# Four scalars in one tile, a filler at the top of memory, weight loads two steps later and more generator steps in the first chunk

## The chip, the cores and the metric

One Trainium2 chip, one of its cores. The metric is the device time of one execution of the whole program in microseconds; three runs were timed, and one more execution was profiled. "TensorE" multiplies matrices, "VectorE", "ScalarE" and "GpSimd" work on elements, and "SyncE" issues most of the DMA transfers from its queue, called SP below.

## The reference

Three layers in a row, on float32 data; batch 4, sequence 576, model width 512 (8 heads of 64).

```python
# attention, per head; only scores within tau of the row's maximum stay
scores = scale * q @ k.T
scores = where(scores >= max(scores) - tau, scores, -1e9)
attn = softmax(scores);  x = attn @ v
# mixing over the sequence (rank 32), then a two-matrix block of width 2048
u = x + ((x.T @ U) @ V).T
x = u + relu(u @ w_ch1) @ w_ch2
# gate: causal convolution of 5 taps, sigmoid
out = (sigmoid(conv(x, conv_w)) * (x @ w_val)) @ w_out
```

U, V and the weight matrices arrive as 64-bit floats and are converted on the chip.

## The kernel before

**Stages.** Attention runs first, in 144 slots `s` of 128 query rows (`9 * NP`), with TensorE taking turns at scores, transposes and attention times values. Then comes the dense part: the hidden width of 2048 is worked off in four chunks c = 0..3 of 512 columns. Chunk 0 is plain: `h1` (L902) and `ch` (L960), each by five blocks of up to 512 of the 2304 rows, with matmuls of 512 columns. Chunks 1 to 3 run over three groups j of 768 rows: `first_layer` (L1122) has seven items of 12 matmuls of 384 columns (a product scheme that gets by with seven block products instead of eight), `second_layer` (L1165) has eight groups of 12. Every float32 product is made of three matmuls (high by high, high by low, low by high). The output stage is `val` (L1039) and `proj` (L1068).

**Operands.** The seven operands of a group j are spilled to DRAM during chunk 0 (`spill`, and `combos`, whose lines are L868 to L877) and fetched again by `fetch` (L1097, DMA at L1101) into four places in turn. A fetch is given out when an item has been used, four items ahead.

**Weights.** A row of weights is loaded into one of two buffers `raw` (L159 for `weight_rows`, L182 for `stage_rows`), converted from 64-bit floats in seven operations (`from_f64`: ScalarE at L102, VectorE at L104, L107, L111, L115, L125, GpSimd at L130), and split into a high part (L171, ScalarE) and a low part (L173, GpSimd). For the first matrix of chunks 1 to 3, `combine` (L189 to L209) forms seven sums of blocks instead. L125 is the last reader of `raw`; the next load into that buffer waits for it in the SP queue, and everything behind it on that queue waits too.

**Order.** All of this is written by hand as Python generators: `work.tick()` (L219) takes each of at most four live generators one step further, which means one operation or a pause, and then starts the next in line. So the number of ticks between two matmul groups sets where each operation stands in its engine's queue. Before a load, `wstage` (L137) waits until the buffer before last has been converted. In chunk 0, `tick` (L1008) is called after each group of 12 matmuls: 24 calls while `lot` is set, which is taken away at L1219, and 8 after it, 32 in all. A first-layer item gives one tick (L1161), a group of the second layer two (L1181). `need` (L808) and L1131 give ticks until the rows are there.

**Memory.** Tiles take whole multiples of 32 bytes per partition, from byte 16,512 upwards in the order of the code: idn 512, then four scalars of 32 each (4 bytes used), cw 96 (80 used), u, ring, w1_0, w2_0 and everything after them, so u begins at 17,248, 96 past a multiple of 256. Pools with `side="right"` are laid out downwards from byte 229,344, which is 224 past a multiple of 256. The sizes of the large tiles are multiples of 256. So before, everything large on the left side begins at 96 past a multiple of 256 (u, w1_0, w2_0, raw, wt, wf, the combined weights w1_s, h2), and on the right side at 224 (the region with its operands, us, w2_1, the tiles of q and k). The identity idn begins at 16,512, 128 past one.

Of the kernel before, what the change touches and what calls it, by code (L numbers as in the profile page):

```python
# [21 lines left out]
F32 = mybir.dt.float32  # L22
# [14 lines left out]
def attention_moe_kernel(  # L37
# [24 lines left out]
    NP = B * H // 2  # L62
# [14 lines left out]
    def f(ap):  # L77
        return ap.bitcast(F32)

    const = ctx.enter_context(tc.tile_pool(name="const", bufs=1))  # L80
    idn = const.tile([128, 128], F32, name="idn")
    tau_sb = const.tile([128, 1], F32, name="tau_sb")
    ntau = const.tile([128, 1], F32, name="ntau")
    tau_eff = const.tile([128, 1], F32, name="tau_eff")
    qscale = const.tile([128, 1], F32, name="qscale")
    cw = const.tile([128, KC, KD], F32, name="cw")
    u = const.tile([128, KD, T], F32, name="u")
    ring = const.tile([128, 1280], F32, name="ring")

    w1_0 = const.tile([128, 2, KD, FC], F32R, name="w1_0")  # L90
    w2_0 = const.tile([128, 2, KD, FC], F32R, name="w2_0")
    wst_p = ctx.enter_context(tc.tile_pool(name="wst", bufs=2))
# [42 lines left out]
    slot = [0]  # L135

    def wstage(n):  # L137
        k = len(started)
        started.append(k)
        while k - len(loaded) >= 2:  # L140
            yield
        raw = wst_p.tile([128, FC, 2], I32, tag="raw", name="raw")
        return raw[:, 0:n, :]
# [104 lines left out]
    work = Staged(4)  # L248
# [13 lines left out]
    def attention(dense_front, dense_mid, dense_back):  # L262
# [388 lines left out]

        nu = 5 * R
        raw_uv = [next_of(wstage(n)) for n in (FC, nu + S - FC)]
        nc.gpsimd.memset(raw_uv[0][:, 0:nu], 0)
        rv = [a.rearrange("p a b -> p (a b)") for a in raw_uv]
# [132 lines left out]
    p1 = {}  # L788
# [54 lines left out]
    def spill(n, t):  # L843
        for j in range(NG):
            for half in range(2):
                a = 2 * G * j + G * half
                lo, hi = max(a, n * NB), min(a + G, n * NB + size[n])
                if lo < hi:
                    for o, k in (((B11, 0), (B21, 2)) if not half else ((B22, 2),)):
                        for p in range(2):  # L850
                            nc.sync.dma_start(
                                out=spilled[j, o][:, p, :, lo - a:hi - a],
                                in_=f(t[:, p, k:k + 2, lo - n * NB:hi - n * NB]))
# [31 lines left out]
    def split_block(src, pool=None):  # L885
        for t in split_steps(src, pool):
            pass
        return t

    def u_src(n):  # L890
        return [(0, size[n], u[:, :, n * NB:n * NB + size[n]])]
# [10 lines left out]
    def h1(c, us, n, apart=False):  # L902
        m = size[n]
        t = p1["h2"] if n == 2 else block_tile(1 + (n + (n > 2)) % 2)
        for e in range(KD):
            ps = p1["a"].tile([128, 512], F32, tag="a", name="a")
            passes(ps, w1[c % 2][0], us, e, m)
            if apart:
                yield t
            nc.scalar.activation(out=t[:, 0, e, 0:m], in_=ps[:, 0:m], func=ACTF.Relu)  # L910
            nc.vector.scalar_tensor_tensor(
                out=t[:, 1, e, 0:m], in0=ps[:, 0:m], scalar=0.0, in1=f(t[:, 0, e, 0:m]), op0=ALU.max, op1=ALU.subtract
            )
            if not apart:
                yield t
# [41 lines left out]
    def dense():  # L957
# [27 lines left out]
        def gate_step():  # L985
            if len(ended) < len(tapped) and tapped[len(ended)] not in gates:
                b, e = tapped[len(ended)]
                g = gate(b, e)
                nc.scalar.activation(out=g, in_=g, func=ACTF.Sigmoid)
                ended.append((b, e))  # L990
            if not gates or gates[0][0] > 1 and "g" not in p1:
                return
            if gates[0] not in tapped:
                return tap(*gates[0])
            b, e = gates[0]
            k = tap_no[0]
            g = gate(b, e, k, S - k)
            nc.vector.scalar_tensor_tensor(
                out=g, in0=u[:, e, b * S:(b + 1) * S - k], scalar=cw[:, KC - 1 - k, e:e + 1], in1=g,
                op0=ALU.mult, op1=ALU.add  # L1000
            )
            if k == 2 and len(gates) > 1 and not (gates[1][0] > 1 and "g" not in p1):
                tap(*gates[1])
            tap_no[0] = k % (KC - 1) + 1
            if k == KC - 1:
                gates.pop(0)

        def tick(n=1):  # L1008
            work.tick()
            turn["w"] ^= 1  # L1010
            if turn["w"] and "lot" not in p1:
                work.tick()
            for _ in range(n):
                gate_step()
            if p1.get("lots"):
                p1["lot"](p1["lots"].pop(0))
# [15 lines left out]
        turn = {"o": 0, "w": 0}  # L1032
# [62 lines left out]
        fetched, used = [], [0]  # L1095

        def fetch(n):  # L1097
            while len(fetched) < min(n, len(stream)):
                _, j, o = stream[len(fetched)]
                t = operands[len(fetched) % 4]  # L1100
                nc.sync.dma_start(out=f(t), in_=spilled[j, o])  # L1101
                fetched.append(t)
# [3 lines left out]
        def low_parts(left=0):  # L1106
            while len(lows) > left:
                src, hi, lo = lows.pop(0)
                nc.vector.scalar_tensor_tensor(  # L1109
                    out=lo, in0=src, scalar=0.0, in1=f(hi), op0=ALU.max, op1=ALU.subtract)  # L1110

        def relu_sum(ps, x, o, k, half):
            hi, lo = (hs[:, a, k, half * G:(half + 1) * G] for a in range(2))
            nc.vector.tensor_tensor(out=o, in0=ps, in1=x, op=ALU.add)  # L1114
            nc.scalar.activation(out=hi, in_=o, func=ACTF.Relu)  # L1115
            lows.append((o, hi, lo))

        def bank(n):
            pool, tag = (c_ps, "c") if n % 2 else (p1["a"], "a")
            return pool.tile([128, 512], F32, tag=tag, name=tag)[:, 0:G]  # L1120

        def first_layer(c, j):  # L1122
            sb = [p1["c"][:, n * G:(n + 1) * G] for n in range(8)]

            def add(ps, x, o):
                nc.vector.tensor_tensor(out=sb[o], in0=ps, in1=sb[x], op=ALU.add)

            for i in range(7):
                t = fetched[used[0]]
                while (c, i) not in summed:  # L1130
                    work.tick()  # L1131
                for m in range(2):
                    ps = bank(m)
                    k = 0
                    for kk in range(2):
                        wh, wl = (parts[i][:, a, kk, m * 128:(m + 1) * 128] for a in range(2))
                        for lhs, rhs in ((wh, t[:, 0, kk]), (wh, t[:, 1, kk]), (wl, t[:, 0, kk])):
                            nc.tensor.matmul(ps, lhs, rhs, start=k == 0, stop=k == 5)  # L1138
                            k += 1
                    if i == 0:  # L1140
                        nc.scalar.activation(out=sb[m], in_=ps, func=ACTF.Copy)  # L1141
                    elif i == 1:
                        add(ps, m, 2 + m)
                    elif i == 2:
                        add(ps, 2 + m, 4 + m)
                    elif i == 3:
                        relu_sum(ps, sb[4 + m], sb[6 + m], 2 + m, 1)
                        add(ps, 2 + m, 2 + m)
                    elif i == 4:
                        relu_sum(ps, sb[2 + m], sb[2 + m], m, 1)  # L1150
                    elif i == 5:
                        relu_sum(ps, sb[m], sb[m], m, 0)
                    else:
                        relu_sum(ps, sb[4 + m], sb[4 + m], 2 + m, 0)
                    low_parts(1)
                used[0] += 1
                if j == NG - 1:
                    freed[0] += 1
                fetch(used[0] + 4)
                for _ in range(1):  # L1160
                    work.tick()  # L1161
                if c == NCH - 1:
                    gate_step()
# [38 lines left out]

        p1["lot"] = lot
        p1["lots"] = [3, 3, 2, 2, 1, 1, 1, 2, 1, 1, 1, 2, 1, 1, 1, 1, 1, 1, 1, 1, 1, 1]
        for n in range(2, NN):
            for t in h1(0, us, n):
                tick()
            held.append((n, t))
            if n + 1 < NN:
                us = split_block(u_src(n + 1))  # L1210
                spill(n + 1, us)
            else:
                fetch(2)
            ch(0, *held.pop(0))
# [75 lines left out]
```

## Time and profile before

| | us |
|---|---|
| median of 3 runs | 837.14 (836.63 to 837.53) |
| the profiled execution | 836.76 |
| its span, first to last instruction | 835.0 |
| TensorE busy | 809.7 (97%) |
| VectorE busy | 682.3 (82%) |
| ScalarE busy | 441.1 (53%) |
| GpSimd busy | 270.2 (32%) |
| mean granted clock of TensorE | 0.993 |

The page gives each engine's busy time as a share of the span, the span in 40 slices, the DMA queues, the chain of work that ended last, and the costliest groups of instructions. Engines are written PE (matmuls), PEld (weight loads into TensorE, beside the matmuls), DVE, ACT, POOL and SP, in the order TensorE, VectorE, ScalarE, GpSimd, SyncE. Matmul records overlap, because the next one starts before the last one's end: the rate is read from one start to the next. A line such as L1176 is a line of the kernel before.

### The profile page before, as it was taken

To read this page: it belongs to the slowest core of one execution; us is meant where nothing else is said; L and a number is where in the kernel's file an instruction comes from. 1 tells how busy PE (TensorE), PEld (TensorE's weight loads), DVE (VectorE), ACT (ScalarE), POOL (GpSimd) and SP (SyncE) were. 2 spreads that over 40 slices of the span, in tenths; PEclk is the share of its full clock that TensorE was granted. 3 is DMA by queue.
4 is the path that set the end of the run, shared out by engine and by line. 5 is a ranking of instruction groups with operands and counts; after the bars stand their busy time and mean duration, and the time that the engine had idled before them with its cause. 6 is when DMAs were issued, how large, how long until landed. Compare 5 with 4: busy or idle time off the path is not lost. (4 is left out here: it accounts for less than half of the span.)

```text
span 835.0 us, 15123 instructions
## 1 busy us (share of the span) xinstructions
PE 809.7 (97%) x5264; PEld 726.3 (87%) x5264; DVE 682.3 (82%) x1414; ACT 441.1 (53%) x929; POOL 270.2 (32%) x362
## 2 busy tenths in 40 slices
PE   8999999999999999999998999999899999999998
PEld 8788888888888887888888998999899999978886
DVE  7999999999999984479977799588896897977740
ACT  6788888888888884344232224213342252344531
POOL 6724523622432420242762167015561310000000
PEclk9999999999999999999999999999989999999999
DMA  7766776685676524476675755559365473001112
GB/s 147 183 145 150 176 166 145 147 185 130 154 169 142 122 50 165 141 266 230 221 271 197 245 191 220 202 179 333 116 266 205 161 265 114 1 1 50 52 51 75
DMA packets 87397, 134.19 MB, mean 161 GB/s; under 512 B 45669, under 2 KB 62837, under 8 KB 87322
## 3 DMA queue, kind: packets, MB, share of 16 engines
q1 hardware_dynamic: 85130, 130.92, 53.1%
q0 software_dynamic: 848, 1.92, 0.9%
q8 instruction: 42, 0.69, 0.3%
q10 hardware_dynamic: 1344, 0.39, 0.2%
q14 instruction: 33, 0.27, 0.1%
HBM read 85.43 MB, written 21.23 MB: 128 GB/s over the span
## 5 line engine op out<-in xcount | busy, mean ns | idle before, releaser
L494 POOL TENSOR_TENSOR th<-nm,tau_eff 128x1 f32<-128x1 f32 x144 | 69.9, 485 | 177.2 <-DVE ns L479 170.2
L504 DVE SCALAR_TENSOR_TENSOR e<-ns,th,e 128x576 f32<-128x576 f32 x144 | 124.3, 863 | 1.4 <-POOL th L494 0.4
L493 ACT ACTIVATE e<-ns,nm 128x576 f32<-128x576 f32 x144 | 112.0, 778 | 20.4 <-DVE ns L479 20.2
L479 DVE TENSOR_SCALAR_CACHE_REDUCE ns<-s 128x576 f32<-128x576 f32 x144 | 107.6, 748 | 9.1 <-PE s L465 8.3
L130 POOL TENSOR_TENSOR wf<-wf,wt 128x512 f32<-128x512 f32 (+2 forms) x43 | 60.7, 1411 | 142.4 <-DVE wt L125 141.7
L465 PE MATMUL s<-st 128*128 128x288 f32 x480 | 93.9, 317 | 0.1
L520 PE MATMUL xm<-idn,e 128*128 128x128 f32 x576 | 86.5, 273 | 2.5 <-DVE e L504 2.4
L1176 PE MATMUL a<-region,w 128*128 128x384 f32 x432 | 84.2, 340 | 4.8 <-ACT w L171 2.1
L1138 PE MATMUL a<-region,w_s 128*128 128x384 f32 x378 | 78.9, 344 | 8.8 <-DMA region<-sp 6.9
L529 ACT ACTIVATE pt<-xm 128x512 f32<-128x512 f32 x144 | 85.7, 595 | 1.6
L1176 PEld LDWEIGHTS a<-region,w 128*128 128x128 f32 x432 | 76.4, 190 | 7.1 <-DVE region L1109 3.2
L1176 PE MATMUL c<-region,w 128*128 128x384 f32 x432 | 81.6, 337 | 0.0
L465 PEld LDWEIGHTS s<-st 128*128 128x128 f32 x480 | 67.9, 189 | 11.9 <-issue 4.2
L1138 PE MATMUL c<-region,w_s 128*128 128x384 f32 x378 | 77.6, 341 | 0.0
L1138 PEld LDWEIGHTS a<-region,w_s 128*128 128x128 f32 x378 | 68.0, 192 | 10.9 <-issue 5.1
L1115 ACT ACTIVATE region<-c_sb 128x384 fp32r<-128x384 f32 x72 | 37.6, 524 | 75.0 <-DVE c_sb L1114 75.0
L1176 PEld LDWEIGHTS c<-region,w 128*128 128x128 f32 x432 | 76.4, 189 | 0.0
L520 PEld LDWEIGHTS xm<-idn,e 128*128 128x128 f32 x576 | 69.3, 140 | 4.4 <-PE s L465 2.3
L574 PE MATMUL o<-pt,vt 128*64 128x256 f32 (+1 forms) x768 | 69.8, 331 | 0.0
L1138 PEld LDWEIGHTS c<-region,w_s 128*128 128x128 f32 x378 | 68.1, 190 | 0.0
L574 PEld LDWEIGHTS o<-pt,vt 128*64 128x64 f32 x768 | 41.4, 137 | 24.5 <-issue 10.3
L102 ACT ACTIVATE wt<-raw 128x512 f32<-128x512 f32 (+2 forms) x43 | 28.4, 665 | 49.4 <-DMA raw<-in_moe_w_ch_dram 45.1
(162 smaller groups left out, 1564.6 us busy)
## 6 DMA issues: line engine op xcount, KB each, us to landing
region<-sp SPq DMA_DIRECT2D x63, 768.0 KB, 6.0
raw<-in_moe_w_ch_dram SPq DMA_DIRECT2D x32, 512.0 KB, 4.2
sp<-c_sb SPq DMA_DIRECT2D x24, 384.0 KB, 3.3
st<-qk SPq DMA_DIRECT2D x30, 256.0 KB, 3.6
st<-qk SPq DMA_DIRECT2D x15, 432.0 KB, 4.1
st<-qk SPq DMA_DIRECT2D x45, 144.0 KB, 3.8
out_dram<-c_sb SPq DMA_DIRECT2D x17, 256.0 KB, 2.0
st<-qk SPq DMA_DIRECT2D x15, 288.0 KB, 5.0
```

The costliest lines, as they stand in the source:

```text
L130: nc.gpsimd.tensor_tensor(out=dst, in0=dst, in1=tf, op=ALU.add)
L465: nc.tensor.matmul(s[:, n, 0:HS], lhs, rhs[:, n * HS:(n + 1) * HS], start=(m == 0), stop=(m == len(ops) - 1))
L479: nc.vector.tensor_scalar(out=ns.rearrange("p (a b) -> p a b", a=2), in0=s, scalar1=-1.0, scalar2=3.0e38, op0=ALU.mult, op1=ALU.min, accum ...
L493: nc.scalar.activation(out=row(p, i), in_=d["ns", i], func=ACTF.Exp, bias=nm[:, 0:1], scale=-1.0)
L494: nc.gpsimd.tensor_tensor(out=th, in0=nm, in1=tau_eff, op=ALU.add)
L504: nc.vector.scalar_tensor_tensor(out=e, in0=d.pop(("ns", i)), scalar=d.pop(("th", i))[:, 0:1], in1=e, op0=ALU.is_le, op1=ALU.mult, accum_o ...
L520: nc.tensor.transpose(x[:, j * 128:(j + 1) * 128], e[:, c + j * 128:c + (j + 1) * 128], idn)
L529: later(s + 1, 0, lambda: nc.scalar.activation(out=dst, in_=x.rearrange("p (j c) -> p j c", j=4), func=ACTF.Copy), "x")
L574: nc.tensor.matmul(o, lhs, rhs, start=False, stop=stop)
L1115: nc.scalar.activation(out=hi, in_=o, func=ACTF.Relu)
L1138: nc.tensor.matmul(ps, lhs, rhs, start=k == 0, stop=k == 5)
L1176: nc.tensor.matmul(ps, lhs, rhs, start=k == 0, stop=k == 3 * KD - 1)
```

## The change

Three things. The four scalars tau_sb, ntau, tau_eff and qscale become columns of one tile of 32 bytes, so that everything after them begins 96 bytes lower, at 17,152 = 67 x 256 for u; and a filler of 56 floats (224 bytes) is allotted first on the right side, so that its tiles begin 224 bytes lower, at multiples of 256. In `wstage`, a load that is given out after slot 144, so every weight load of the dense part, pauses two steps more. In `tick`, a list of 32 entries, 1 and 2 in turn, gives the number of ticks per call, where before the first 24 calls gave one each and the later ones two and one in turn; after the list the rule is that of before. The `- 0` at the fetch changes nothing.

```diff
-    tau_sb = const.tile([128, 1], F32, name="tau_sb")
-    ntau = const.tile([128, 1], F32, name="ntau")
-    tau_eff = const.tile([128, 1], F32, name="tau_eff")
-    qscale = const.tile([128, 1], F32, name="qscale")
+    scalars = const.tile([128, 8], F32, name="scalars")
+    tau_sb, ntau, tau_eff, qscale = (scalars[:, n:n + 1] for n in range(4))
...
+    ctx.enter_context(tc.tile_pool(name="pad", bufs=1, side="right")).tile([128, 56], F32, name="pad_top")
     w1_0 = const.tile([128, 2, KD, FC], F32R, name="w1_0")
...
         while k - len(loaded) >= 2:
+            yield
+        for _ in range(2 * (slot[0] > 9 * NP)):
             yield
...
         def tick(n=1):
-            work.tick()
             turn["w"] ^= 1
-            if turn["w"] and "lot" not in p1:
+            for _ in range(p1["ticks"].pop(0) if p1.get("ticks") else 1 + turn["w"]):
                 work.tick()
...
-                fetch(used[0] + 4)
+                fetch(used[0] + 4 - 0)
...
+        p1["ticks"] = [1, 2, 1, 2, 1, 2, 1, 2, 1, 2, 1, 2, 1, 2, 1, 2, 1, 2, 1, 2, 1, 2, 1, 2, 1, 2, 1, 2, 1, 2, 1, 2]
```

## Rows read from the trace of the kernel before

**Rows 1.** The page, busy us, share and instructions of each engine
```profile
PE 809.7 (97%) x5264; PEld 726.3 (87%) x5264; DVE 682.3 (82%) x1414; ACT 441.1 (53%) x929; POOL 270.2 (32%) x362
```
**Rows 2.** Windows, dense part: stretch and length, busy by engine, clock, DMA share, GB/s
```profile
345.09:423.18 78.09, 78.09 (x385) 65.59 (x384) 63.50 (x97) 28.55 (x55) 38.87 (x29) 1.00 0.62 214
423.18:462.38 39.20, 34.03 (x182) 32.79 (x181) 29.62 (x56) 10.32 (x19) 13.35 (x11) 0.96 0.63 232
...
494.35:528.15 33.80, 32.54 (x182) 31.25 (x182) 27.31 (x43) 11.24 (x22) 18.98 (x13) 1.00 0.50 179
...
561.73:593.99 32.26, 31.95 (x182) 31.58 (x182) 27.54 (x50) 9.34 (x17) 16.04 (x12) 1.00 0.70 252
593.99:632.69 38.70, 34.27 (x182) 33.98 (x182) 36.05 (x54) 14.04 (x26) 25.63 (x18) 0.91 0.49 184
...
697.06:728.49 31.43, 31.43 (x182) 31.43 (x182) 26.60 (x45) 11.71 (x19) 0.00 (x0) 1.00 0.22 76
```
**Rows 3.** Timeline of TensorE: start, length, operation, count, [idle before, who ended it]
```profile
436.05 1.29 PE L1138 MATMUL a<-region,w_s 128*128 128x384 f32 x6 [1.81 <-DVE c_sb L1114]
...
443.14 0.62 PE L1176 MATMUL a<-region,w 128*128 128x384 f32 x2 [2.10 <-ACT w L171]
444.93 2.58 PE L1176 MATMUL a<-region,w 128*128 128x384 f32 x7 [1.17 <-POOL w L173]
...
539.52 1.30 PE L1138 MATMUL a<-region,w_s 128*128 128x384 f32 x6 [0.65 <-DMA region<-sp]
...
607.02 2.26 PE L1138 MATMUL a<-region,w_s 128*128 128x384 f32 x6 [4.43 <-DMA region<-sp]
609.08 2.12 PE L1138 MATMUL c<-region,w_s 128*128 128x384 f32 x6
```
**Rows 4.** Timelines of SP and VectorE near 600 us; SP's waits (total, times, longest)
```profile
591.06 10.78 SPq L159 DMA_DIRECT2D raw<-in_moe_w_val_dram  x3
601.94 1.33 SPq L1101 DMA_DIRECT2D region<-sp  x3
...
600.76 0.68 DVE L125 SCALAR_TENSOR_TENSOR wt<-raw,wt 128x512 f32<-128x512 uint32 x1
...
SPq L159 <- DVE wt L125: 79.3, 16, 10.3
```
**Rows 5.** Windows, only instructions on the conversion's tile wt: DVE, ACT, POOL busy
```profile
561.73:593.99 32.26, 14.18 (x21) 2.67 (x4) 6.83 (x5) 1.00 0.70 252
593.99:632.69 38.70, 17.92 (x22) 2.68 (x4) 7.05 (x5) 0.91 0.49 184
```
**Rows 6.** The chain that ended last, in order of time: start, us, what
```profile
620.18 2.11 PE a L1176 x12
...
666.33 1.06 PE c L1138 x6
...
682.66 2.08 PE c L1176 x12
...
752.51 11.19 PE p L1076 x48
```
**Rows 7.** Timeline of TensorE, first chunk: from one start to the next
```profile
356.24 11.32 PE L899 MATMUL c<-region,w 128*128 128x512 f32 x48
367.40 11.32 PE L899 MATMUL a<-region,w 128*128 128x512 f32 x48
...
395.41 11.04 PE L899 MATMUL c<-h,w 128*128 128x512 f32 x48
406.29 17.05 PE L899 MATMUL c<-region,w 128*128 128x512 f32 x96
```
**Rows 8.** Timeline of ScalarE at the start
```profile
3.57 0.20 ACT L646 ACTIVATE ntau<-idn 128x1 f32<-128x1 f32 x1
...
6.35 0.60 ACT L361 ACTIVATE qk<-tm 128x512 fp32r<-128x512 f32 x1 [2.58 <-PE tm L392]
```

## The prediction

> **What bounds the kernel now.** I read the page's busy table first [rows 1]: TensorE is busy in 809.7 of 835.0 us, so time can only come from its 25 us of idle, from stretches at a lower clock, or from matmuls that themselves run slower than they could. To see where, I cut the dense part into windows [rows 2]: the first chunk (345 to 423 us), then windows of one (c, j) pair each, of which five are shown; I call them c1j0 (423 to 462), c1j2 (494 to 528), c2j1, c2j2 (594 to 633) and c3j2 (697 to 728). All nine pairs have the same 180 matmuls of weights by operands. c3j2 takes 31.43 us and TensorE never waits in it, so that is the price of a pair with nothing in its way. c1j0 takes 39.20, c2j2 38.70, c1j2 33.80: they lose 7.8, 7.3 and 2.4 us. In the first chunk TensorE has no gap at all, while VectorE is busy in 63.50 of 78.09 us.
>
> The timeline of TensorE says what is waited for [rows 3]. In c1j0: 1.81 us for VectorE's additions, then 2.10 and 1.17 us for the two operations that finish the last weight row of chunk 1's second matrix. In c2j2: 4.43 us for an operand fetch. After each long wait the clock is lower: six matmuls from 607.02 need 2.06 us to the next group, twice the 1.06 of a full-speed group [rows 6], and the granted clock of these windows is 0.96 and 0.91 against 1.00. So the losses of 7.8 and 7.3 are the waits plus what the clock gives up behind them.
>
> Why the fetch was late stands in the SP queue [rows 4]: three weight loads occupy it from 591.06 to 601.84, each waiting until VectorE's L125 has read the buffer that it overwrites (the third for the L125 of 600.76), and the fetches start behind them at 601.94. Over the kernel SP stands 79.3 us in this wait. VectorE is late because the conversions come in a crowd: 14.18 and 17.92 us of conversion in c2j1 and c2j2 [rows 5], beside its own work there (8 updates of u, 22 operations on c_sb and the region).
>
> **The change part by part.** *Ticks.* Counting calls of tick() in the code: 24 in the first chunk while "lot" is set and 8 after. Before, they give 24 + 12 = 36 steps of the generators; after, 48. The new delay costs each pair of loads (two raw buffers) two steps: chunk 1 has four pairs, 8 steps. Net 12 - 8 = 4 steps earlier at the end of chunk 1's weights. I followed the generators step by step through both versions: the last L173 of the second matrix is given out after item 6 of c1j0 before, and after item 2 now. Each item is 2.11 us, so 8.4 us earlier, while TensorE waited for it until 444.93 [rows 3]. The first waits go with it, since VectorE's five conversion steps of that row also leave c1j0. What is late next there: nothing that I find; conversions given out within c1j0 fall from five to three. I take 7.3 of the 7.8 us (bounds 5.1, the three waits alone, and 7.8).
>
> The price is in the first chunk: 48 steps instead of 36 bring some 1.3 more conversions before 423 us. In c2j2 22 operations on the conversion's tile take 17.92 us [rows 5], so five of them 4.1 us, and 1.3 conversions 5.3 us. VectorE idles 78.09 - 63.50 = 14.6 us there [rows 2], and TensorE writes into four buffers per pool, so a late addition of some us is covered. Cost nothing; if that cover were gone, up to 5.3 us.
>
> *Loads two steps later.* The load of a raw buffer is given out two steps after the L125 that frees it (two items, 4.2 us, in a first layer; one block of u, 2.1 us, in a second) instead of in the same or the next step. Everything behind a load on SP (operand fetches, spills) moves ahead of it by that much. Following the steps, the loads of w_val that blocked at 591 to 602 come 10 to 21 us later in program order: the first after item 0 of c2j2, the second after item 3, the third and fourth in c2j2's second layer, where SP has no fetch to make. The conversions also spread: conversions that end in c2j1 fall from five to four, in c1j1 from five to four, and c1j2, c2j2 get one more each. Of c2j2's 7.3 us I take 5.0 (bounds 0 and 7.3): the first w_val load still stands before two fetches that TensorE needs. For c1j2 I take 0 (bounds 2.4 either way: less carried in, one more conversion inside). The short fetch waits (0.65 us at 539.52 [rows 3], and three more like it) keep their cause, a weight load sharing the DMA engines with fetches; the loads move by two items, so I take 0, bounds 1.5 either way. No need() or summed wait of the code gets a forced step in my count: w_out's last row is ready in c3j1.
>
> *Tiles at multiples of 256 bytes.* Before, all left-hand tiles begin at 96 past a multiple of 256 and all right-hand ones at 224; after, all at 0. In the trace this seems to matter for TensorE. Second-layer groups of 12 matmuls (384 columns) take 2.08 us in c3 (682.66), where weights (w2_1) and operand are both at 224, and 2.11 in c2 (620.18), where the weights (w2_0) are at 96 [rows 6]. The same with 512 columns: 48 matmuls from h2 (at 96, weights at 96) take 406.29 - 395.41 = 10.88 us, from the region (224 against 96) 367.40 - 356.24 = 11.16 [rows 7], and 11.19 in the output stage [rows 6], where weights and moving operand are at 224 and 96. So unequal places seem to cost 2.5 ns per matmul of 384 and 5.8 to 6.5 of 512 columns. Counts from the code: 756 first-layer matmuls (all unequal: 1.06 us for six is the slow rate), 288 second-layer ones of chunk 2, 528 wide ones of L899 and 216 of L1076. Sum 1044 x 2.5 ns + 528 x 5.8 + 216 x 6.5 = 2.6 + 3.1 + 1.4 = 7.1 us, all on TensorE's path. No row shows two tiles both at 0; I take 7.1 because both equal pairs that the rows show (96 with 96, 224 with 224) are fast. Bounds: 0 and 7.1. The identity stays at 128, so transposes get no equal place; no row shows them faster or slower by it.
>
> The trace shows 11.16 against 10.88 us for the same 48 matmuls. The Trainium skill (SBUF — State Buffer, Who interferes with whom) says that TensorE has two independent read ports, one for the moving operand and one for weight loads, and never waits on anyone; by that, places can't matter and this part is worth 0. The rows speak against it so far.
>
> *One tile for four scalars.* If its parts were ordered as one, the first activation (L646, 3.57 us) would wait for tau to land. ScalarE idles 2.58 us before its next work at 6.35 [rows 8], so nothing is lost; without that cover, under a microsecond once.
>
> Sum on the profiled execution (836.76 us, of which 1.76 lie outside the span; 0.38 under the median of 837.14): 836.76 - 7.3 - 5.0 - 7.1 = 817.4; on the median 817.7.
>
> **The rivals.** *A: places don't matter for TensorE*, the 2.08 and 2.11 having another cause that goes with the chunk. Only the waits go: 817.7 + 7.1 = 824.8. The Trainium skill's section named above would expect this one (SBUF — State Buffer, Who interferes with whom). For it: no row varies the place alone. Against: it holds for three kinds of matmul with different partners.
>
> *B: the hole of c2j2 moves instead of closing.* The first w_val load, after item 0, waits for an L125 given out one step pair earlier; VectorE then runs behind its program by some us, and the fetches for items 5 and 6 stand behind the load. Price up to the 5.0 that I took off: 822.7. It decides if VectorE is more than 4.2 us (two items) behind.
>
> *C, slower: loads now stand among first-layer fetches.* Three of them do (conv_w in c1j0, the first load of chunk 3's second matrix after item 1 of c2j1, w_val's first after item 0 of c2j2). If each blocks SP as in rows 4, each costs what c2j2 lost: 3 x 7.3 = 21.9 us, in place of the 7.8 + 7.3 that go, and with nothing from the places: 837.1 + 6.8 = 843.9. It decides from the same point, an L125 more than 4.2 us late at each of them. Against it: each of them now comes two steps after its L125 and not in the same one, and two of the three follow stretches with four conversions, not five.
>
> *D: the change doesn't do what it says.* The 96 bytes saved below and the pad of 224 above put every large tile at a multiple of 256 by plain addition, so that can't fail; but the ticks could be eaten by the delay, so that c1j0 stays as it is (817.7 + 7.3 = 825.0, as in A). My count of 12 against 8 speaks against that.
>
> **How the numbers follow.** Forecast 817.7 with chance 0.62 (812.5 to 820.5 with the bounds of the small terms); A or D 0.17; B 0.10; a gain beyond 812.5 0.03; two of A, B and D with parts of C, which cancel to within 0.2% 0.03; C 0.05. The range 812.5 to 827 takes in the forecast, A, B and D and leaves out both ends and the last two. Faster by over 0.2% (1.7 us, about what a measurement of this kernel can tell from no change) 0.92, within 0.2% 0.03, slower 0.05.
>
> **What would show it.** Ticks: c1j0 near 31.5 to 32 us, no wait for L171 or L173 in it. Loads: c2j2 under 34 us, SP never 10 us in L159 before c2j2's fetches, granted clock 1.00 there. Places: 2.08 us per 12 matmuls in chunk 2 as in 1 and 3, first-layer groups of six at 1.04, 48 wide matmuls at 10.88 from the region and in the output stage. Wrong if first-layer pairs get new fetch waits of several us, if VectorE delays TensorE in the first chunk, or if the window after 728 us, which has no loads, is not some 2.5 us shorter.

## The result, and the profile after

The changed kernel takes 822.70 us (median of four runs, 821.95 to 823.84) against 837.34 (836.63 to 838.53) of the kernel before beside it: a ratio of 0.9825, 95% interval 0.9807 to 0.9843. Its profiled execution took 823.84 us, with a span of 822.1.

In the new kernel most lines up to L1000 stand one higher or lower than before (L899 is L900, L125 is L124, L159 is L160, L171 and L173 are L172 and L174, L966 is L967); from L1076 on they are the same.

The page's busy table of the changed kernel, beside [rows 1]:

```profile
PE 801.9 (98%) x5264; PEld 723.1 (88%) x5264; DVE 679.3 (83%) x1414; ACT 441.1 (54%) x929; POOL 268.0 (33%) x362
```

Windows of the changed kernel, in the columns of [rows 2]: the first chunk, c1j0, c1j2, c2j1, c2j2, c3j2, and the output stage:

```profile
344.49:430.60 86.11, 79.80 (x386) 67.44 (x384) 67.22 (x101) 30.29 (x58) 42.90 (x32) 0.96 0.65 223
430.60:462.72 32.12, 31.48 (x183) 31.19 (x182) 27.70 (x53) 8.60 (x16) 8.17 (x7) 1.00 0.62 222
494.46:527.99 33.53, 32.10 (x181) 31.02 (x181) 27.43 (x46) 12.06 (x23) 20.85 (x14) 1.00 0.49 192
559.60:591.97 32.37, 31.57 (x181) 31.11 (x181) 26.95 (x51) 8.82 (x16) 13.66 (x10) 1.00 0.64 235
591.97:623.28 31.31, 31.31 (x182) 31.16 (x181) 28.14 (x44) 12.81 (x24) 20.07 (x15) 1.00 0.64 239
686.70:717.93 31.23, 31.23 (x181) 31.22 (x181) 26.91 (x47) 12.06 (x20) 0.00 (x0) 1.00 0.22 77
717.93:822.07 104.14, 99.05 (x457) 82.10 (x456) 60.33 (x102) 41.20 (x71) 0.00 (x0) 1.00 0.12 46
```

The two holes are gone: c1j0 fell from 39.20 to 32.12 us, c2j2 from 38.70 to 31.31, both at a clock of 1.00. But the first chunk, where TensorE had no gap, now takes 86.11 us instead of 78.09, at 0.96. The timeline of TensorE shows where, and that the matmuls themselves are faster; its columns are those of [rows 3] and [rows 7]:

```profile
355.37 11.04 PE L900 MATMUL c<-region,w 128*128 128x512 f32 x48
366.25 11.04 PE L900 MATMUL a<-region,w 128*128 128x512 f32 x48
...
411.14 19.62 PE L900 MATMUL c<-region,w 128*128 128x512 f32 x96 [6.31 <-DVE u L967]
...
598.21 1.20 PE L1138 MATMUL a<-region,w_s 128*128 128x384 f32 x6
599.25 1.20 PE L1138 MATMUL c<-region,w_s 128*128 128x384 f32 x6
...
606.64 2.24 PE L1176 MATMUL a<-region,w 128*128 128x384 f32 x12
608.72 2.24 PE L1176 MATMUL c<-region,w 128*128 128x384 f32 x12
```

From one start to the next, 48 matmuls from the region take 10.88 us (11.16 in [rows 7]), six of a first layer 1.04 (1.06 in [rows 6]) and twelve of a second layer in chunk 2 2.08 (2.11). One wait of 6.31 us for VectorE's addition L967 is new, and the 96 matmuls behind it take 19.46 us to the next group, 2.6 more than the 16.89 of before [rows 7] (to 423.18).

SP before c2j2, in the timeline and the list of its waits (in total, times, longest), beside [rows 4]: no load occupies it for 10 us any more, and its waits for the conversion fell from 79.3 to 53.6 us.

```profile
581.58 3.10 SPq L160 DMA_DIRECT2D raw<-in_moe_w_ch_dram  x2
...
594.67 0.37 SPq L160 DMA_DIRECT2D raw<-in_moe_w_val_dram  x1
...
SPq L160 <- DVE wt L124: 53.6, 11, 9.2
```

What goes on behind the new wait stands in the timelines of ScalarE, VectorE and GpSimd of the changed kernel:

```profile
383.75 0.67 ACT L101 ACTIVATE wt<-raw 128x512 f32<-128x512 f32 x1 [1.90 <-DMA raw<-in_moe_w_ch_dram]
386.10 0.53 ACT L872 ACTIVATE c_sb<-ring 128x384 fp32r<-128x384 f32 x1 [1.69 <-DMA sp<-c_sb]
...
386.66 0.56 DVE L877 TENSOR_TENSOR c_sb<-ring,c_sb 128x384 fp32r<-128x384 f32 x1 [3.62 <-ACT c_sb L872]
...
401.78 1.65 DVE L869 TENSOR_TENSOR ring<-u,ring 128x384 f32<-128x384 f32 x1
403.35 0.41 DVE L912 SCALAR_TENSOR_TENSOR region<-a,region 128x256 fp32r<-128x256 f32 x1
403.68 1.32 DVE L877 TENSOR_TENSOR c_sb<-ring,c_sb 128x384 fp32r<-128x384 f32 x1
...
399.95 6.17 POOL L200 TENSOR_TENSOR wf<-wf 128x512 f32<-128x512 f32 x4
```

Two things are to be seen. At 381.9 us ScalarE comes to a conversion (L101) whose raw load lands only at 383.75; everything behind it in ScalarE's queue waits, and VectorE stands idle for 3.62 us. The raw load is not all of that: L101 ends at 384.42, and ScalarE's next operation, L872, stands 1.69 us more until a store of c_sb has landed. Then, around 400 us, VectorE's operations of the combinations (L869, L877) take 1.3 to 1.65 us each where they took 0.55, while GpSimd runs the sums of chunk 1's first matrix (L200). In the kernel before, in the same timelines of GpSimd and VectorE, L868 takes 0.55 us at 396 us, and the sums (L199) come at 402 to 408 us, behind all but the last combinations:

```profile
402.22 6.00 POOL L199 TENSOR_TENSOR wf<-wf 128x512 f32<-128x512 f32 x4
...
396.07 0.55 DVE L868 TENSOR_TENSOR ring<-u,ring 128x384 f32<-128x384 f32 x1
```

So the sums came only 2.3 us sooner (399.95 against 402.22). That they met the combinations is also due to the stop: VectorE's first L869 of that group starts at 389.33 us, 3.1 us later than before (386.27).

The stages of most kernels that follow, in us, each from the first matmul of a stage to the first of the next, the output stage to the end of the span (one profiled execution each):

| stage | before | after | places only | old ticks | no delay | old places | sums held | held, loads sooner | 17 single ticks |
|---|---|---|---|---|---|---|---|---|---|
| first chunk | 78.1 | 86.1 | 77.1 | 76.8 | 92.7 | 85.4 | 82.1 | 78.2 | 87.2 |
| c1j0 | 39.2 | 32.1 | 39.0 | 52.1 | 32.7 | 31.5 | 34.2 | 34.7 | 31.6 |
| c1j1, c1j2 | 65.8 | 65.3 | 65.7 | 65.6 | 66.6 | 65.4 | 64.9 | 65.1 | 65.0 |
| c2j0, c2j1 | 65.8 | 64.0 | 65.8 | 63.7 | 66.2 | 63.5 | 63.3 | 63.3 | 64.1 |
| c2j2 | 38.7 | 31.3 | 39.3 | 31.6 | 38.8 | 31.9 | 31.5 | 31.6 | 31.5 |
| chunk 3 | 95.8 | 94.7 | 95.5 | 94.7 | 94.8 | 94.7 | 94.4 | 95.0 | 95.4 |
| output | 106.5 | 104.1 | 104.1 | 104.1 | 104.1 | 106.5 | 104.2 | 104.1 | 104.1 |

### The profile page after: what moved, and what is told of

It is laid out like the page before. It is cut to its first block, busy times and chain, and to the rows that moved or that the text cites. A ratio compares the mean times of both kernels' runs of the same rounds, so it can differ in the third digit from the quotient of the medians.

```text
span 822.1 us, 15122 instructions
## 1 busy us (share of the span) xinstructions
PE 801.9 (98%) x5264; PEld 723.1 (88%) x5264; DVE 679.3 (83%) x1414; ACT 441.1 (54%) x929; POOL 268.0 (33%) x362
## 4 chain that ended last, share of the span: by engine, by line
PE 79%; DVE 10%; DMA 4%; issue 3%; ACT 3%; POOL 1%; ACTq 0%; SPq 0%; DVEq 0%; POOLq 0%
PE s L466 9%; PE o L575 8%; PE c L1176 8%; PE a L1176 8%; PE xm L521 7%; PE p L1076 6%; PE a L1138 6%; PE v L900 6%; PE c L1138 5%; PE a L900 3%; PE c L900 2%; PE o L564 2%; DMA sp<-c_sb 2%; PE t L614 2%; PE tm L393 1%
## 5 line engine op out<-in xcount | busy, mean ns | idle before, releaser
L495 POOL TENSOR_TENSOR th<-nm,scalars 128x1 f32<-128x1 f32 x144 | 69.4, 482 | 178.2 <-DVE ns L480 171.2
L1176 PE MATMUL a<-region,w 128*128 128x384 f32 x432 | 81.3, 335 | 0.6 <-DVE region L1109 0.5
L1138 PE MATMUL a<-region,w_s 128*128 128x384 f32 x378 | 76.5, 337 | 2.9 <-DVE c_sb L1114 1.1
L1138 PE MATMUL c<-region,w_s 128*128 128x384 f32 x378 | 75.7, 334 | 0.0
L1138 PEld LDWEIGHTS a<-region,w_s 128*128 128x128 f32 x378 | 65.8, 188 | 5.0 <-DVE region L1109 2.0
L1138 PEld LDWEIGHTS c<-region,w_s 128*128 128x128 f32 x378 | 66.5, 188 | 0.0
L172 ACT ACTIVATE w<-wf 128x512 fp32r<-128x512 f32 x28 | 17.7, 631 | 70.5 <-POOL wf L129 70.4
```

The source lines that it names most:

```text
L495: nc.gpsimd.tensor_tensor(out=th, in0=nm, in1=tau_eff, op=ALU.add)
L1176: nc.tensor.matmul(ps, lhs, rhs, start=k == 0, stop=k == 3 * KD - 1)
```

## The experiments: one part at a time

The theory at this point: the places speed up TensorE everywhere, the delay closes the hole of c2j2, the ticks that of c1j0, and the ticks also make the new hole. The first four kernels each do or undo one part; the kernel before, run beside them, took 836.91 us.

**Places alone**: the kernel before with the new tile and the filler.

```diff
-    tau_sb = const.tile([128, 1], F32, name="tau_sb")
...
+    scalars = const.tile([128, 8], F32, name="scalars")
...
+    ctx.enter_context(tc.tile_pool(name="pad", bufs=1, side="right")).tile([128, 56], F32, name="pad_top")
```

> The kernel before with the tiles moved to multiples of 256 bytes and nothing else. If the places set TensorE's rate: 837.3 - 7.1 = about 830, first-layer items 2.08 us instead of 2.11, output stage 104.1 instead of 106.5 us, and the waits of c1j0 and c2j2 as before. If the places do nothing and the rate of the changed kernel comes from the calmer queues: 837, items 2.11 us.

832.83 us, ratio 0.9951 (0.9934 to 0.9969). The rates are those of the changed kernel, but the whole gain is 4.1 us, not 7.1. The table says where: 1.0 us in the first chunk, 2.4 in the output stage, and in all nine pairs together 0.1, though 2.6 was due there (another 0.6 lies ahead of the first chunk, which begins at 344.51 us instead of 345.09). In pairs with waits the faster matmuls only come sooner to what they wait for, as in c2j2 of this kernel (4.43 us in [rows 3]; L1137 is L1138 here):

```profile
605.43 2.26 PE L1137 MATMUL a<-region,w_s 128*128 128x384 f32 x6 [4.98 <-DMA region<-sp]
```

**Ticks of before**: the changed kernel with one tick in each of 24 calls, then two and one in turn.

```diff
-        p1["ticks"] = [1, 2, 1, 2, ...
+        p1["ticks"] = [1] * 24 + [2, 1] * 4
```

> The changed kernel with the ticks per call of before. If the additional ticks make the new wait in the first chunk: that chunk takes about 76 us instead of 86 and TensorE never waits in it, while the second matrix of chunk 1 is now late (8 ticks are given at once before the second layer of c1j0, which then loses 8 to 14 us): 820 to 826 in all, c2j2 stays near 31.3. If the wait comes from the later loads or the faster TensorE, the first chunk stays near 86 us and the whole goes above 830.

834.07 us, ratio 0.9962 (0.9947 to 0.9977). The first chunk is at 76.8 us without a wait, so the hole there comes with the ticks. c1j0 costs 52.1, worse than expected and than before the change: with the delay and without the ticks, the second matrix is later than it ever was, and a fetch is late too.

```profile
431.15 2.26 PE L1138 MATMUL a<-region,w_s 128*128 128x384 f32 x6 [5.48 <-DMA region<-sp]
...
449.87 1.01 PE L1176 MATMUL a<-region,w 128*128 128x384 f32 x2 [5.72 <-ACT w L172]
```

So beside the delay the ticks are worth 20.0 us in c1j0 and cost 9.3 in the first chunk.

**No delay**: the changed kernel without its two steps.

```diff
-        for _ in range(2 * (slot[0] > 9 * NP)):
-            yield
```

> The changed kernel without the two steps before each load. If the delay closes the hole of c2j2: c2j2 goes back to 36 to 38.5 us with SP held in L159 for some 10 us before its fetches, the first chunk keeps its wait (12 ticks more and no step given back), about 829 in all. If the hole closed because the faster TensorE or the earlier chunk moved it, c2j2 stays near 31.3 and the whole is 822 or less.

842.45 us, ratio 1.0064 (1.0045 to 1.0083): slower than before. The timelines of TensorE and SP (lines stand two lower here):

```profile
417.66 19.73 PE L898 MATMUL c<-region,w 128*128 128x512 f32 x96 [11.37 <-DVE u L965]
...
616.16 2.26 PE L1136 MATMUL a<-region,w_s 128*128 128x384 f32 x6 [4.84 <-DMA region<-sp]
...
600.13 10.75 SPq L158 DMA_DIRECT2D raw<-in_moe_w_val_dram  x3
```

The hole of c2j2 is back (38.8 us), with the same three loads ahead of the fetches: the delay closes it. The miss is in the first chunk: without the delay the ticks put still more conversions into it (40 of VectorE's operations on the tile wt, against 34 in the changed kernel), and its wait grows to 11.37 us. The delay is a part of the first chunk's sum, which I had counted for c1j0 alone.

**Old places**: the changed kernel with four tiles for the scalars and no filler.

> The changed kernel with the tiles where they were before. If places are worth 7.1 us and independent of the rest: 829.8, items 2.11 us, output stage 106.5. The wait in the first chunk stays (near 88 us for the chunk) if it comes from the ticks; it goes if a faster TensorE is what outran VectorE there.

827.04 us, ratio 0.9881 (0.9860 to 0.9901): 4.3 us by the medians over the changed kernel (7.1 expected). The output stage is back at 106.5 us. The first chunk is at 85.4 with a wait of 5.58 us for the same addition, so faster matmuls didn't make the hole.

## The experiments: what a place is

**Both at 96**: the kernel before with a filler of 32 floats on the right side.

```diff
+    ctx.enter_context(tc.tile_pool(name="pad", bufs=1, side="right")).tile([128, 32], F32, name="pad_top")
```

> The kernel before, with 32 floats more on the right side only, so that weights and activations both begin 96 bytes past a multiple of 256 instead of at places that differ. If what counts for a matmul is that its two operands lie at the same place modulo 256: 173.3 ns for 384 columns in the wide stages, and a time like that of the run with only the places changed, 832 to 834. If only multiples of 256 bytes give the gain: rates stay at 175.8 to 176 and the time at 836 to 838.

834.05 us, ratio 0.9953 (0.9936 to 0.9970), the same as with places at 0 within the interval. Multiples of 256 aren't needed; equal places do as well.

**64 and 32 apart**: fillers of 16 and 24 floats.

> The kernel before, with 16 floats more on the right side: weights 96 and activations 160 bytes past a multiple of 256, 64 apart. If equality is needed: 175.8 to 176 ns per 384-column matmul and an output stage of 106.5 us. If being apart by 64 does as well: 173.3 ns and 104.1 us.

> The kernel before, with 24 floats more on the right side: weights 96 and activations 128 bytes past a multiple of 256, 32 apart, as far apart as tiles can be put by one step. If every difference costs the same: the 48 matmuls of 512 columns in the output stage at 11.19 us between starts, output stage 106.0 to 106.5. If only larger differences cost: 10.88 and 104.1.

The timelines of TensorE in the output stage (L1077 is L1076 here), first of the kernel with both at 96, then 64 apart, then 32 apart. From start to start, 48 matmuls take 10.88, 11.20 and 11.21 us:

```profile
772.03 11.04 PE L1077 MATMUL p<-w,region 128*128 128x512 f32 x48
782.91 11.04 PE L900 MATMUL v<-region,w 128*128 128x512 f32 x48
```

```profile
766.34 11.36 PE L900 MATMUL v<-region,w 128*128 128x512 f32 x48
777.54 11.36 PE L1077 MATMUL p<-w,region 128*128 128x512 f32 x48
```

```profile
774.95 11.37 PE L1077 MATMUL p<-w,region 128*128 128x512 f32 x48
786.16 11.36 PE L900 MATMUL v<-region,w 128*128 128x512 f32 x48
```

The times, 839.35 and 836.89 us (one run each), are those of the kernel before, and the output stages take 106.0 and 106.5. For these 48 matmuls, being 32 or 64 bytes apart costs what 128 cost.

For 384 columns the expectation failed. The first layer of c1j0 in the timeline of the kernel 64 apart:

```profile
424.14 1.20 PE L1139 MATMUL c<-region,w_s 128*128 128x384 f32 x6
425.18 1.20 PE L1139 MATMUL a<-region,w_s 128*128 128x384 f32 x6
```

Six take 1.04 us, the rate of equal places (173.3 ns each), and so do nearly all first-layer groups of this kernel at full clock; twelve of chunk 2's second layer take 2.08. At 32 apart they take 1.06 (1.04 in a part of chunk 1's groups) and 2.12. The 512-column matmuls of the first chunk lie between at 64 apart, 10.99 us per 48, and 48 matmuls of 256 columns there go the other way: 5.75 us with the places at 0, 5.65 at 64 and 5.60 at 32 apart. So equal places were fast in every kernel for 384 and 512 columns, but being apart is not by itself what costs: it depends on the distance and the width, and these runs don't show why.

## The experiments: the hole of the first chunk

Three theories. T1: GpSimd's sums beside VectorE's combinations slow these. T2: VectorE simply has too much conversion in the chunk. T3: it starts with ScalarE's stop for a late raw load.

**Sums held**: the changed kernel, the sums given out only when the combinations are.

```diff
-        while len(rows_in) < KD:
+        while len(rows_in) < KD or "lot" in p1:
```

> The changed kernel, but GpSimd's sums of the first weight matrix of chunk 1 (L200 to L207) are not given out before the last operand combinations of stage j=2 have been given out; the ticks, the delay and the places stay as in the changed kernel. Theory T1 (the hole of the first chunk comes from GpSimd's sums running beside VectorE's combinations: the one class of operations slows the other): the first chunk falls from 86.1 us to 76 to 78, no wait over 2 us of TensorE for VectorE's L967 in it, VectorE's 256-column subtractions stay near 0.55 to 0.7 us, whole time 813 to 816. Rival T2 (VectorE has simply more conversion work than fits there): conversions come as before, so the wait stays, first chunk 84 to 88, whole time 821 to 824. Rival T3 (ScalarE's stop at L101 for a raw load near 383 us starts the backlog): the same stop stays, first chunk 84 to 88. Bad turn for all: the sums come so late that the first six products of chunk 1 wait for them, first pair of chunk 1 35 to 38 instead of 32.1.

821.94 us, ratio 0.9814 (0.9789 to 0.9839), by the medians within the scatter of the changed kernel. In the profiled execution the first chunk fell by 4.0 us to 82.1, between the numbers of all three theories. Timelines of VectorE and TensorE:

```profile
386.16 0.56 DVE L877 TENSOR_TENSOR c_sb<-ring,c_sb 128x384 fp32r<-128x384 f32 x1 [3.56 <-ACT c_sb L872]
...
400.51 0.55 DVE L869 TENSOR_TENSOR ring<-u,ring 128x384 f32<-128x384 f32 x1
...
407.63 18.55 PE L900 MATMUL c<-region,w 128*128 128x512 f32 x96 [3.36 <-DVE u L967]
```

L869 is back at 0.55 us with GpSimd idle, so the slowing that T1 names is real. Its worth is less certain: 4.0 us of the first chunk in one profiled execution each, of which c1j0 gives back 2.0, since the sums come later; the whole time lies where T2 had it. The idle 3.56 us before 386.16 and a wait of 3.36 remain.

**Sums that only write**: the four operations of L200 as fills; their arithmetic is left out.

```diff
-            nc.gpsimd.tensor_tensor(out=o, in0=x, in1=y, op=op)
+            nc.gpsimd.memset(o, 0.0)
```

> The changed kernel, but GpSimd's four subtractions and additions of L200 are fills, which read nothing (this arithmetic is left out: the products of chunk 1 and after use wrong sums). The splits of L207 on GpSimd stay. Under T1 with the sums' reads as the cause: VectorE's combinations of 400 to 410 us fall from 1.3 to 1.66 us to about 0.55 to 0.7, and the first chunk falls by 4 to 9 us, to 77 to 82. Under T2 and T3 the first chunk stays at 84 to 88 and the durations too.

One run, 820.44 us; first chunk 84.4, so the gain was smaller than T1 said (1.7 us; 84 to 88 was the range of T2 and T3), and the early idle stayed. The durations beside L200 went as T1 expected; the splits of L207 still read. Timelines of GpSimd and VectorE:

```profile
399.99 1.92 POOL L200 MEMSET wf<- 128x512 f32 x4
...
401.18 0.55 DVE L869 TENSOR_TENSOR ring<-u,ring 128x384 f32<-128x384 f32 x1
```

**Later ticks**: 17 calls with one tick and 15 with two; and 20 calls with one.

```diff
+        p1["ticks"] = [1] * 17 + [2] * 15
```

```diff
+        p1["ticks"] = [1] * 20 + [2, 2] + [3, 2] * 5
```

> The changed kernel with another list of ticks: one in each of the first 17 calls, two in each of the last 15 (47 in all instead of 48). Theory T4, after the run that held the sums (first chunk 82.1, half of the hole gone, with VectorE still stopped for 3.6 us at 382.6 by ScalarE's conversion that waits for its raw load): the hole has two parts, conversions given out sooner than their raw loads land, and sums beside combinations; both come from ticks in the first 17 calls, so a list that keeps to one there has neither: first chunk 76.5 to 79, no wait over 2 us for VectorE in it, first pair of chunk 1 at 32 to 34, whole time 813 to 817. Rival T2 (VectorE has too much conversion work for the first chunk as a whole): the hole moves to the end of the chunk, 82 to 86, whole time 819 to 824.

> The changed kernel with one tick in each of the first 20 calls and 2 to 3 in the last 12 (49 in all). T4: first chunk 76.5 to 78; the second matrix is ready no later than with 17 and 15, so the first pair of chunk 1 at 32 to 34; whole time 812 to 816. If three ticks in a call of half width bunch VectorE's conversions ahead of its additions: waits of TensorE for L967 at the end of the first chunk, 79 to 83, whole time 816 to 820. T2: 82 to 86.

824.76 us (0.9844, 0.9824 to 0.9863) and 823.30 (0.9825, 0.9802 to 0.9848), first chunks of 87.2 and 85.5: the hole moved to the end of the chunk, as T2 said, but not for its reason. ScalarE, VectorE and TensorE in the first of the two:

```profile
414.36 0.66 ACT L101 ACTIVATE wt<-raw 128x512 f32<-128x512 f32 x1 [10.46 <-DMA raw<-in_moe_w_ch_dram]
...
415.06 0.43 DVE L103 TENSOR_SCALAR wt<-wt 128x512 f32<-128x512 f32 x1 [6.83 <-ACT wt L101]
...
422.52 2.93 PE L900 MATMUL c<-region,w 128*128 128x256 f32 x12 [4.17 <-DVE u L967]
```

VectorE isn't full there, it stands idle for 6.83 us behind a conversion whose raw load is late, with TensorE's additions queued behind it. ScalarE reached this conversion at 403.90, before SP gave out the load (404.61, behind stores of c_sb and operand fetches), and the load landed 9.75 us later. With two ticks to a call, half as many calls lie between a load and its conversion as with one. That is T3, in another place; T4's claim that late ticks have neither cause fell.

**Sums held and loads sooner**: for chunk 1, the two steps of delay put behind the load instead of before it (`soon` is set while the first chunk runs); conversions keep their ticks.

```diff
-        for _ in range(2 * (slot[0] > 9 * NP)):
+        for _ in range(2 * (slot[0] > 9 * NP and not soon)):
             yield
         raw = wst_p...
...
-        for _ in range(4):
+        for _ in range(4 + 2 * len(soon)):
...
-        while len(rows_in) < KD:
+        while len(rows_in) < KD or "lot" in p1:
```

> The changed kernel with both stops of the first chunk addressed: GpSimd's sums held until the last combinations are given out (as in the run that held them alone), and, for the two matrices of chunk 1, the two steps of delay put behind the load instead of before it, so that every conversion is given out at the same tick as in the changed kernel and only the raw loads two ticks sooner. Theory T3 (beside T1: ScalarE's conversion L101 stops near 382 us for a raw load given out at 378 and landed at 383.75, VectorE stands idle behind it for 3.6 us, and this backlog is the other half of the hole): against the run that held the sums alone, VectorE's idle of 3.56 us at 382.6 goes, the wait of 3.36 us for L967 goes, the first chunk falls from 82.1 to 76.5 to 78.5, whole time 811 to 815, the fastest of all. If the raw loads are not the other half: first chunk stays at 81 to 83, whole time 818 to 821. Bad turn: raw loads that come sooner get among the spills and block SyncE, first chunk over 84.

817.93 us (816.99 to 818.67), ratio 0.9766 (0.9749 to 0.9782): the fastest kernel of the study, 4.8 us under the changed one. The first chunk is at 78.2. ScalarE and TensorE:

```profile
383.67 0.66 ACT L101 ACTIVATE wt<-raw 128x512 f32<-128x512 f32 x1
...
405.94 16.93 PE L900 MATMUL c<-region,w 128*128 128x512 f32 x96 [1.13 <-DVE u L967]
...
423.83 0.97 PE L1138 MATMUL a<-region,w_s 128*128 128x384 f32 x4 [0.62 <-POOL w_s L207]
```

L101 waits for no load, and the wait for L967 is 1.13 us. From 86.1 to 82.1 by holding the sums, and to 78.2 by the sooner loads on top: the two together account for 7.9 of the 9.0 us that the chunk lies above the kernel with the places alone (77.1). VectorE's idle of 3.56 us became 1.56 there; L872 still waits for a store of c_sb. The time stays above the 811 to 815 that I expected; c1j0 costs 34.7 us instead of 32.1, and 0.62 of that is a wait for the sums that were held. The loads sooner without the sums held were not tried, and since the stop is part of why sums and combinations meet, the shares of the two causes aren't settled.

T2 falls. Windows of the first chunk, only instructions on the conversion's tile wt, in the columns of [rows 5], of the kernel before, the changed one and this one:

```profile
345.09:423.18 78.09, 22.57 (x30) 3.89 (x6) 8.51 (x5) 1.00 0.62 214
344.49:430.60 86.11, 20.77 (x34) 5.09 (x8) 8.93 (x6) 0.96 0.65 223
344.46:422.70 78.24, 21.22 (x33) 5.20 (x8) 8.93 (x6) 1.00 0.68 239
```

The changed kernel has four more of VectorE's conversion operations in its first chunk than the kernel before, and they take less time; this kernel has nearly as many and no long wait. What takes longer in the changed kernel are VectorE's 32 combination operations (L869, L877): 26.8 us against 21.3 before and 20.2 here.

## Why the prediction was right or wrong

**The whole.** The forecast was 817.7 us, the time is 822.7: inside the range, on the side forecast, and 5.0 us off. It is the number of rival B to the decimal, but not B's mechanism: c2j2's hole closed. That it is only 5.0 off is in part luck: the 9.0 us of the first chunk (below) and the 3.0 that the places fell short were met in part by 2.4 more in c2j2 and some 3.5 in pairs that I had taken at 0.

**First chunk: the step that failed.** I wrote "Cost nothing; if that cover were gone, up to 5.3 us". The chunk grew by 8.0 us although faster matmuls give it 1.0, so the price was 9.0; "if VectorE delays TensorE in the first chunk" was a sign of being wrong, and it came. The conversions that I priced weren't what cost: the trace has four more of VectorE's operations on wt, 0.8 of a conversion and not 1.3, and 1.8 us less of VectorE's time in them. I had found the cover in two averages, 14.6 us of VectorE idle in the window [rows 2] and four buffers per pool. Windows of the kernel before, cut finer than [rows 2] and in its columns, show where VectorE's idle time lay:

```profile
345.00:360.00 15.00, 15.00 (x67) 12.14 (x66) 6.45 (x11) 6.08 (x12) 5.61 (x5) 1.00 0.42 143
...
390.00:400.00 10.00, 10.00 (x68) 9.22 (x68) 10.00 (x22) 3.83 (x9) 2.34 (x1) 1.00 0.56 195
...
420.00:432.00 12.00, 11.90 (x78) 11.59 (x77) 7.62 (x15) 3.58 (x8) 8.59 (x7) 1.00 0.65 243
```

It was idle in the first 15 us and around the end, and busy for all of the 10 us from 390 on, where the ticks brought more. I moved the conversions by ticks and gave them a duration, but didn't follow what else the same ticks move: the four L200 of GpSimd, and the time that a raw load has to land before ScalarE stands at it.

The rows of VectorE and GpSimd say what the sums do: 0.55 us becomes 1.3 to 1.65 for L869 and L877, which read two tiles of SBUF, while L912, which reads PSUM and one tile, stays at 0.41 between them; with fills in place of the sums it is 0.55 again. The Trainium skill (SBUF — State Buffer, Who interferes with whom) states this as a rule: a VectorE instruction with two SBUF inputs contends with a GpSimd instruction that reads SBUF, not with one that only writes it. The trace agrees in all three respects. I had weighed its neighbour, on TensorE, and not this one.

**Ticks in c1j0**: 7.3 us taken, 7.1 measured, no wait for L172 or L174. Right in the path: with the old ticks these waits are there, larger. The count was too good: I had the conversions within c1j0 fall from five to three, and in the trace VectorE's operations on wt there, five to a conversion, fell from 25 to 22.

**Delay**: 5.0 taken for c2j2, 7.4 measured, at the upper bound. The first w_val load that I feared stands in SP for 0.37 us. I had one conversion more in c2j2; VectorE's operations on wt there fell from 22 to 16. The three pairs that I took at 0 gained little in c1j2 (0.3), but c2j0 and c2j1 together 1.9, and these two lose it again without the delay (66.2 against 64.0).

**Places**: the rates were right for every kind of matmul, and "both equal pairs are fast" held for the third. The term was mis-sized for the whole: 7.1 us taken, 4.1 measured alone and 4.3 undone; "all on TensorE's path" is what failed in it. In the output stage, with no loads, 2.4 of 2.5 arrived; in the pairs of the kernel before 0.1 of 2.6; where TensorE waits there, as in c2j2, what it waits for doesn't come sooner. Rival A (worth nothing) fell. The rows disagree with what the prediction drew from two independent read ports and a TensorE that never waits (the Trainium skill, SBUF — State Buffer, Who interferes with whom), that places can't matter: 10.88 against 11.16 to 11.21 us for the same 48 matmuls.

**Rivals C and D** fell: no first-layer pair got a fetch wait over a microsecond, and c1j0 changed. The scalars' tile cost nothing that shows: the attention stage ends at 344.49 us, before 345.09.

The sum with measured terms, against the span of 835.0: attention -0.6, first chunk +8.0, c1j0 -7.1, c1j1 and c1j2 -0.5, c2j0 and c2j1 -1.9, c2j2 -7.4, chunk 3 -1.2, output -2.4, together -13.1, with 12.9 between the spans (the terms are rounded). The medians lie 14.6 apart: the profiled execution of the changed kernel was the slowest of its four.

## What to carry to other kernels

Work moved into an engine's idle time must be placed in the timeline, not in a window's average: look at what the other engines run at that moment, above all GpSimd reading SBUF beside VectorE's two-input operations, and at whether the loads that it reads have landed. When several generators share a tick, a list of ticks moves all of them, so follow each one's DMAs and each queue behind them. A faster matmul pays in full only in stages where TensorE waits for nothing; elsewhere it pays after the waits are gone.

## What the runs showed of the hardware

How fast TensorE multiplies depends on where weights and moving operand begin modulo 256 bytes. 48 matmuls of 512 columns take 10.88 us at equal places (0 and 0, 96 and 96) and 11.16 to 11.21 at 32 and 128 bytes apart; at 64 apart they take 10.99 in the first chunk and 11.00 to 11.20 in the output stage. Twelve of 384 columns take 2.08 us at equal places and at 64 apart, 2.11 to 2.12 at 128 and 32 apart. VectorE's 128x384 subtraction of two SBUF tiles takes 0.55 us alone and up to 1.65 beside GpSimd's, and is not slowed by GpSimd's fills. After the wait of 6.31 us the granted clock was 0.69 from 411.14 to 420.60 us (0.96 over the whole chunk), and the matmuls behind the wait took 2.6 us longer, so this hole cost more than its wait, as in c1j0 and c2j2 before.
